# A replanned instruction order, key-row sums in halves, and GpSimd waiting for small VectorE groups, in a fused attention and expert kernel

## The chip, the cores and the metric

The kernel runs on 1 core of one Trainium2 chip. The metric is the device time of one execution in microseconds (us), as the median over several executions. Engines: TensorE (PE in the profile; PEld is its weight load), VectorE (DVE), ScalarE (ACT), GpSimd (POOL), and SyncE (SP), which issues most of the DMAs.

## The reference

Four batches of 12,288 query rows (128 wide) attend to 768 keys each. The keys are means over 4x4 patches of `kv`, times `w_sr`, and they are the values too. The result feeds a mixture of 8 experts in which each row uses its best expert alone:

```python
kv_pool = kv.reshape(B, H // r, r, W // r, r, C).mean(axis=(2, 4))
k = v = kv_pool.reshape(B, -1, C) @ w_sr
s = scale * (q @ k.transpose(0, 2, 1))
a = softmax(s);  x = (a @ v).reshape(B * S, D)
logits = x @ w_gate;  e = argmax(logits);  gate = softmax(logits)[e]
y = gate[:, None] * (relu(x @ w1[e]) @ w2[e])
```

## The kernel before

The queries are cut into 96 blocks of 512 rows (24 for each batch), numbered t. For a block the kernel computes:

- scores: 3 pairs of 512-column matmuls (`s`), ScalarE's exponential (`e`, line 974) and a VectorE operation of 1024 columns (`r`, line 976) which takes e away from 1 + s;
- values: 36 small matmuls into `po` from `r` and from a 128x128 matrix `M` of the batch;
- `x` in two float16 parts: either ScalarE (line 1010) and VectorE (1011) make them, or ScalarE copies `po` (1013) and GpSimd makes both parts (1014, 1016); a transposing DMA turns them (1022);
- the hidden layer of the one expert that the batch is guessed to use: three units of 128 hidden columns (`ph`), ScalarE's ReLU (1045, 1053), the first unit split in two parts by GpSimd (1047, 1049);
- the output `py`: for each of 4 chunks of 128 rows, 3 matmuls with `L`, 2 with the split unit, and one for each unit used; VectorE applies the gate (1080), and a DMA stores.

The queries' own two parts are made by GpSimd (955, 957) and turned by a DMA (959).

For a third unit there is a choice for each block, the way `u{t}`. Without it, the unit's four output matmuls are made. With it, they are left out (`UB = UH - 1`), and ScalarE's ReLU of that unit also sums its result into a flag (line 1057, with an extra instruction that reads the accumulator), which later decides whether the block's rows stand. Other ways choose the engine of one copy: `x{t}` for the two parts of `x`, `l{t}` for the logits' copy (ScalarE line 1018 or VectorE line 1020), `a`, `b`, `c` for the key parts and weights of a batch.

Once per batch there is other work among the blocks. `keys` loads 12 pieces of `kv`; GpSimd adds four rows of each of 3 groups (`rows_sum`, line 443, 1024 columns each; batches 1 to 3 only), halves them twice more (447, 455), and PE turns and multiplies them. `expert` guesses the expert (576 to 580), makes gate weights relative to it (`relative`, 584 to 588), loads the two weights (625, 626), and sorts and gathers hidden units in many small steps. `marks` and `count_steps` (1421 to 1424) gather the rows that the shortcut does not cover; `general_step` can compute 128 such rows exactly, and is placed once after each of the first three batches.

The order of all of it is made by a planner, `Plan`, when the kernel is built. Each `op(engine, us, fn, at, needs, gives, bufs, ...)` has a length `us`, a due time `at`, its needs, and its buffers. `order` simulates the engines with these lengths: at every step it takes, of the operations that can start, the earliest by start and due time. `NUDGE` moves due times, of a kind of operation, of one operation (`=name`) or of one block (`@t`); `WAYS` makes the choices above. An operation with `lock`, and every GpSimd operation, also holds one common lock in the plan, so that no two of these overlap there:

```python
if o.lock:
    start = max(start, locked)
```

`issue` then emits the instructions in the planned order. On the chip each engine runs its instructions in that order, and waits only where data or a buffer demands it: the lock is in the plan alone. Early in the plan (20 to 110 us) PE's empty places are filled with matmuls without use (`fill`, on `slots16`).

Of the kernel before, what the change touches and what calls it, by code (L numbers as in the profile page):

```python
# [17 lines left out]
P = 128  # L18
# [55 lines left out]
pf.48:14.5 pf.72:-14 pl:-52 po.1:1 po.2:0.5 pooled.2:3.5 pt.2.3:4 qh:1.5 qp:2.5 quiet.72:-41.5 r.0:-1 r.1:2.5 r.2:-3
see:-10 some0:20 uy0:-53 vTd.0:11.5 w:-9.5 w2U:11 w2m:-8.5 xf:0.5 xh:0.5 zp:2.5 =D.15:9 =Mh.0:11 =e.23.1:-4.5
=e.36.2:1 =e.38.1:-0.5 =e.38.2:-8.5 =e.49.2:12 =e.5.2:-88.5 =e.52.2:-5.5 =e.54.1:4.5 =e.63.2:-1.5 =e.66.1:-8
=e.67.2:-6 =e.79.1:-23 =e.8.0:10 =e.85.2:-0.5 =e.88.2:3.5 =ex.1:1.5 =ex.8:2 =fl.1:38 =fl.27:4 =fl.56:-21 =fl.75:5
=fl.79:-1.5 =g.2:-1.5 =g.5:10.5 =g.7:-8 =g.71:-6.5 =g.73:-26.5 =gate.12:3 =gate.22:-2 =general.0.done:-5.5
=general.0.s:-3.5 =general.1.ph0:-2 =general.1.ph4:-11 =general.2.find:-0.5 =general.2.h0:-23 =gf.47:1.5 =gf.57:-3.5
=gf.65:-0.5 =gh.3:5.5 =gh.35:3.5 =kp0.2:10 =kt.0:47 =kv.0.2.3:-11.5 =lg.56:-5 =lg.75:-1.5 =lg.76:-5.5 =lg.79:-4.5  # L80
=lgc.10:4.5 =lp.0.0:21.5 =lp.1.24:18 =own2.2:-2 =pL.0:-2.5 =pX.0:-6.5 =perm.2.1:2 =perm.2.4:-1.5 =ph.0.1:5 =ph.0.2:4.5
=ph.16.1:1.5 =ph.21.1:-10.5 =ph.25.1:1 =ph.25.2:-12 =ph.26.0:3 =ph.43.1:0.5 =ph.44.1:8 =ph.48.0:-3 =ph.48.1:-2
=ph.49.1:-8.5 =ph.51.0:6 =ph.52.2:-2 =ph.62.0:-2.5 =ph.79.0:1 =ph.79.1:3 =ph.8.2:-1 =ph.80.2:3.5 =ph.81.0:1 =ph.88.1:1
# [5 lines left out]
=s.21.2:3 =s.22.0:2.5 =s.22.1:-1.5 =s.3.0:-12.5 =s.31.1:-5 =s.32.2:2 =s.33.0:9.5 =s.33.2:-6.5 =s.44.2:-8 =s.46.0:-5.5
=s.52.0:8 =s.61.0:-3 =s.71.0:-2.5 =s.78.2:-6 =s.81.0:-2 =s.88.1:-4.5 =s.88.2:-5.5 =s.9.1:-6 =s.91.1:-2.5 =s.94.1:7  # L90
=s.95.0:-9 =s.95.1:-1.5 =s.95.2:3.5 =se.13:15.5 =some.2:2.5 =unit.3:22.5 =w.7:20.5 =w2l.2:-7.5 =xf.60:6.5 =xf.77:4
=xf.80:2 =xf.88:-11 =xh.29:-18.5 =xh.52:10 =xl.21:5.5 =xl.68:6 =xl.81:28 =xl.87:-10 =ys.10:-5 =ys.20:-32.5 =ys.30:2
=ys.67:3.5 =ys.75:-2.5 @0:1.5 @1:-7.5 @14:-0.5 @15:1 @20:-1.5 @21:1.5 @23:0.5 @24:1 @26:-6 @3:-0.5 @30:-1.5 @31:2
# [3 lines left out]
""".split())}
WAYS = dict.fromkeys("""
a0 a1 a2 b2 c1 c2 c3 l3 l4 l9 l11 l13 l16 l17 l19 l21 l22 l23 l31 l33 l34 l36 l37 l38 l42 l45 l46 l48 l49 l50 l56 l59
l60 l61 l62 l69 l75 l78 l80 l81 l82 l83 l84 l85 l87 l88 l89 l93 u0 u1 u4 u5 u12 u13 u14 u15 u16 u19 u23 u25 u27 u31  # L100
u32 u34 u35 u37 u38 u39 u41 u43 u45 u46 u48 u49 u50 u51 u52 u53 u55 u56 u57 u62 u63 u64 u65 u72 u75 u78 u79 u80 u82
u84 u85 u86 x0 x7 x8 x9 x13 x17 x18 x19 x20 x21 x22 x24 x30 x31 x32 x34 x36 x37 x39 x41 x42 x43 x44 x45 x51 x54 x55
x57 x60 x62 x63 x64 x66 x67 x69 x70 x71 x74 x76 x77 x78 x79 x80 x82 x84 x88 x94
# [12 lines left out]
class Plan:  # L116


    all_ways = False
# [117 lines left out]
@with_exitstack
def attention_moe(ctx: ExitStack, tc, q, kv, w_sr, w_gate, w1, w2, out):
# [164 lines left out]
    def keys(b, when):  # L403
# [6 lines left out]
        for d in range(NK // D):  # L410
# [123 lines left out]
        op("POOL", 1.75, lambda: nc.gpsimd.tensor_sub(kp.tile[:, 1], kt.tile, kp.tile[:, 0]), at + 5, [("kp0", b)],  # L534
# [16 lines left out]
        op("DVE", .3, lambda: nc.vector.scalar_tensor_tensor(M.tile[:, 1, :P], pm.tile[:, :P], cn[:, 9:10], M.tile[:, 0, :P],  # L551
# [11 lines left out]
    def expert(b, at):  # L563
# [3 lines left out]
        op("DVE", .25, lambda: nc.vector.tensor_scalar(cbc.tile, ones, cn[:, 7:8], None, op0=ALU.mult), at,  # L567
# [22 lines left out]
        op("DVE", 1.0, guess, at + .5, [("pg", b)], [("first", b)], [pg, cg])  # L590
        op("DVE", 1.0, relative, at + 2, [("first", b)], [("cg", b)], [cg], lock=True)
# [28 lines left out]
        op("DVE", .4, logits_m, at + 4, [("plg", b), ("M", b)], [("Mx", b), ("v16x", b)], [plg, M])  # L620
# [41 lines left out]
        op("DVE", .5, sides, at + 8.5, [("zc", b)], [("side", b)], [pz, sg])  # L662
# [16 lines left out]
        op("DVE", .8, near, at + 11.5, [("u2", b), ("mir", b)], [("key", b)], [pu, sg], lock=True)  # L679
# [24 lines left out]
        op("DVE", .17, lambda: chosen(0), at + 15, [("less", b, 0)], [("some0", b)], [la, sg])  # L704
        op("DVE", .35, largest, at + 16, [("less", b, 1), ("some0", b)], [("some", b)], [la, sg])
# [48 lines left out]
        op("DVE", .35, limit, at + 35, [("class", b), ("unit", b)], [("Tb", b)], [la])  # L754
# [28 lines left out]
        op("DVE", .85, scales, at + 16, [("pw", b)], [("ws0", b)], [pw, ws])  # L783
        op("POOL", 1.1, scales2, at + 17, [("ws0", b), ("mir", b)], [("ws", b)], [ws, sg])
# [709 lines left out]
```

## Time and profile before

| what | value |
|---|---|
| median of 3 executions | 817.34 us (816.2 to 818.12) |
| profiled execution, its own time | 819.5 us |
| its span, first to last instruction | 817.7 us |
| mean granted TensorE clock | 0.987 |
| PE busy | 759.8 us (93%) |
| VectorE busy | 652.2 us (80%) |
| GpSimd busy | 601.1 us (74%) |
| ScalarE busy | 592.2 us (72%) |

Busy times are sums over the whole span. TensorE's matmuls overlap each other, so that its busy share is no utilization; the granted clock is a share of full speed.

### The profile page before, as it was taken

Reading aid. Unit: us, or ns where it says so; the run is one execution under the profiler, and the core shown is the slowest. Engines: PE = TensorE matmul, PEld = TensorE weight load, DVE = VectorE, ACT = ScalarE, POOL = GpSimd, SP = SyncE. Lnnn points to the kernel's source line nnn. Section 1 sums busy time; section 2 is a strip of 40 time slices with the busy share of each in tenths; the row PEclk is TensorE's granted clock in tenths of the full one; section 3 lists DMA queues with packets and bytes.
Section 4 is the critical chain, followed back from the end, with each engine's and each line's share of the span. In section 5 each row is a group of like instructions: output and inputs, shape, how many; then the busy total and the mean of one; then the engine's idle time right before and its main releaser. Section 6 shows DMA issues by size and latency. Waiting matters only on the chain.

```text
span 817.7 us, 21949 instructions
## 1 busy us (share of the span) xinstructions
PE 759.8 (93%) x8535; PEld 597.3 (73%) x8535; DVE 652.2 (80%) x1224; ACT 592.2 (72%) x949; POOL 601.1 (74%) x802
## 2 busy tenths in 40 slices
PE   5978999999998988999998978999999999999996
PEld 4547777788786766788776756787787777787875
DVE  5767876888877988878979888788896899868684
ACT  1435878778788766877878767888878878788773
POOL 0543599976779978996778788987767888566545
PEclk9989999999999999999999999999999999999999
DMA  9642999894589987897659789979467789757543
GB/s 338 207 99 53 185 210 256 185 208 103 111 212 173 240 201 190 201 172 169 118 138 218 161 208 222 233 166 202 109 127 153 162 165 226 147 116 136 126 84 93
DMA packets 328282, 139.45 MB, mean 171 GB/s; under 512 B 214590, under 2 KB 320194, under 8 KB 328176
## 3 DMA queue, kind: packets, MB, share of 16 engines
q1 hardware_dynamic: 327696, 137.80, 76.4%
q8 instruction: 67, 1.10, 0.6%
q14 instruction: 39, 0.32, 0.1%
q0 software_dynamic: 192, 0.17, 0.1%
q10 hardware_dynamic: 288, 0.07, 0.0%
HBM read 59.12 MB, written 26.94 MB: 105 GB/s over the span
## 4 chain that ended last, share of the span: by engine, by line
PE 62%; DVE 18%; DMA 7%; POOL 6%; issue 3%; ACT 3%; SPq 0%; DVEq 0%; POOLq 0%; ACTq 0%
PE b L353 30%; PE po L353 17%; PE s L353 13%; DVE r L976 8%; DMA qT<-qp 4%; DMA kv<-in_kv_dram 2%; POOL kv L443 2%; DVE y L1080 1%; ACT e L974 1%; DVE junk L1181 1%; DVE xp L1011 1%; POOL g L1049 1%; DMA x<-xp 1%; DVE la L698 1%; DVE PU L746 0%
## 5 line engine op out<-in xcount | busy, mean ns | idle before, releaser
L976 DVE SCALAR_TENSOR_TENSOR r<-s,e 128x1024 bf16<-128x1024 f32 x288 | 346.2, 1215 | 66.5 <-ACT e L974 64.7
L974 ACT ACTIVATE e<-s 128x1024 f32<-128x1024 f32 x288 | 292.5, 1026 | 95.8 <-PE s L353 88.1
L353 PE MATMUL po<-v,r 128*128 128x145 f16 x2304 | 253.7, 228 | 6.7 <-DVE xp L1011 3.2
L353 PE MATMUL s<-qT,KT 128*128 128x512 f16 x576 | 170.5, 384 | 20.1 <-DVE r L976 12.7
L353 PEld LDWEIGHTS <-r 128*128 128x128 bf16 x2304 | 169.1, 99 | 26.9 <-DVE xp L1011 3.8
L353 PE MATMUL b<-w2U,g 128*128 128x128 f16 x1736 | 159.8, 219 | 1.0 <-POOL g L1049 1.0
L353 PE MATMUL b<-x,w1U 128*128 128x512 f16 x465 | 141.9, 381 | 4.2 <-ACT g L1053 1.4
L353 PE MATMUL po<-M,qT 128*128 128x136 f16 x1152 | 131.8, 224 | 0.0
L353 PE MATMUL b<-L,x 128*128 128x128 f16 x1116 | 123.0, 219 | 0.6 <-ACT pT L467 0.3
L1053 ACT ACTIVATE g<-b,zb 128x512 f16<-128x512 f32 x146 | 99.4, 689 | 25.8 <-PE b L353 24.9
L1049 POOL TENSOR_TENSOR g<-X,g 128x512 f16<-128x512 f32 x96 | 112.8, 1175 | 6.5
L957 POOL TENSOR_TENSOR qp<-qr,qp 128x512 f16<-128x512 f32 x94 | 110.4, 1175 | 5.3
L353 PEld LDWEIGHTS <-g 128*128 128x128 f16 x1736 | 113.0, 98 | 1.2 <-POOL g L1049 1.1
L353 PEld LDWEIGHTS <-qT 128*128 128x128 f16 x1152 | 85.4, 98 | 32.2 <-issue 6.9
L353 PEld LDWEIGHTS <-x 128*128 128x128 f16 x1116 | 81.0, 98 | 17.8 <-issue 2.8
L1047 POOL CAST g<-X 128x512 f16<-128x512 f32 x96 | 60.8, 634 | 41.5 <-ACT X L1045 37.5
L353 PEld LDWEIGHTS <-KT 128*128 128x128 bf16 x576 | 51.2, 100 | 53.4 <-issue 23.2
L955 POOL CAST qp<-qr 128x512 f16<-128x512 f32 x94 | 59.1, 630 | 36.7 <-DMA qr<-in_q_dram 25.2
L1080 DVE TENSOR_TENSOR y<-b,gt 128x512 f32<-128x512 f32 x96 | 65.3, 681 | 17.8 <-PE b L353 12.7
L1045 ACT ACTIVATE X<-b,zb 128x512 f32<-128x512 f32 x96 | 66.4, 693 | 16.8 <-PE b L353 16.1
L353 PEld LDWEIGHTS <-w1U 128*128 128x128 f16 x480 | 45.6, 99 | 35.5 <-issue 4.3
L443 POOL TENSOR_TENSOR kv<-kv,kv 128x1024 f32<-128x1024 f32 x27 | 63.6, 2356 | 6.3 <-DMA kv<-in_kv_dram 5.4
(365 smaller groups left out, 992.3 us busy)
## 6 DMA issues: line engine op xcount, KB each, us to landing
qr<-in_q_dram SPq DMA_DIRECT2D x96, 256.0 KB, 3.4
out_dram<-y SPq DMA_DIRECT2D x96, 256.0 KB, 2.8
kv<-in_kv_dram SPq DMA_DIRECT2D x41, 512.0 KB, 6.5
raw<-in_moe_w_dram SPq DMA_DIRECT2D x14, 512.0 KB, 5.5
e<-in_kv_dram SPq DMA_DIRECT2D x3, 512.0 KB, 8.6
v_dram<-vT SPq DMA_DIRECT2D x4, 384.0 KB, 2.9
qT<-qp SPq DMA_TRANSPOSE x94, 3.4
x<-xp SPq DMA_TRANSPOSE x93, 3.5
```

The costliest lines, as they stand in the source:

```text
L353: return nc.tensor.matmul(o, l, r, start=start, stop=stop)
L443: nc.gpsimd.tensor_add(flat(to), flat(to), flat(of))
L698: nc.vector.tensor_scalar(lc(2 + NC * j, NC), limits, lc(j), key(j), op0=ALU.is_ge, op1=ALU.mult)
L955: op("POOL", .62, lambda: nc.gpsimd.tensor_copy(qp.tile[:, 0], qr.tile), T - 1.9 * LEN, [("qr", t)], [("qh", t)], [qr, qp])
L957: op("POOL", 1.17, lambda: nc.gpsimd.tensor_sub(qp.tile[:, 1], qr.tile, qp.tile[:, 0]), T - 1.8 * LEN, [("qh", t)], [("qp", t)], [qr, qp])
L974: op("ACT", 1.03, lambda e=e, ps=ps: nc.scalar.activation(e.tile, ps.tile, AF.Exp), at + .6, [("s", t, s)], [("e", t, s)], [ps, e])
L976: op("DVE", 1.22, lambda e=e, ps=ps, s=s: nc.vector.scalar_tensor_tensor(r.tile[:, 2 * s:2 * s + 2], ps.tile, 1.0, e.tile, op0=ALU.add, op ...
L1045: op("ACT", .69, lambda ph=ph, zu=zu: nc.scalar.activation(gf.tile, ph.tile, AF.Relu, bias=zu()), at + .5, [("ph", t, u), ("zb", b)], [("g ...
L1047: op("POOL", .62, lambda: nc.gpsimd.tensor_copy(gg.tile[:, 0], gf.tile), at + 1.5, [("gf", t)], [("gh", t), ("g", t)], [gf, gg])
L1049: op("POOL", 1.16, lambda: nc.gpsimd.tensor_sub(gg.tile[:, UH], gf.tile, gg.tile[:, 0]), at + 2, [("gf", t), ("gh", t)], [("g", t)], [gf, gg])
L1053: op("ACT", .69, lambda u=u, ph=ph, zu=zu: nc.scalar.activation(gg.tile[:, u], ph.tile, AF.Relu, bias=zu()), at + .5, [("ph", t, u), ("zb" ...
L1080: op("DVE", .69, lambda: nc.vector.tensor_tensor(y.tile, py.tile.rearrange("p (c d) -> p c d", d=C), bc(gr["gt"].tile[:, 0, js], C), op=AL ...
```

## The change

Five things are changed together.

- Many lengths `us` in the plan are replaced by others (some 40 of them), and many groups of small VectorE instructions get `lock=True`.
- `rows_sum` adds 512 columns at a time, twice, instead of 1024 once.
- `issue` adds a real wait: where a locked VectorE operation has more than one instruction, the first GpSimd operation planned after it waits for the last of them, if its planned start lies no later than 2.5 us after the group's planned end.
- The plan lets `ph` of the later units wait for its `g` buffer, and `pL` and `Ls` for `Ms`.
- `NUDGE` and `WAYS` are replaced as a whole. Counted from the diff: `u` is set for 62 blocks instead of 46 (17 dropped, 33 new), `x` for 48 instead of 47, `l` for 45 instead of 41; `a` for batches 0 and 1 instead of 0 to 2; `b` for batches 0 and 3 instead of 2; `c` as before.

```diff
 NUDGE = {...}
-L:16 Lh:26 Tb:0.5 cg:-2.5 drs:-8.5 e.1:1.5 e.2:-0.5 ex:4.5 fl:-0.5 gate:6.5 general.0.pl:-39.5 general.0.pv:5.5
...
+D:1.5 KT:-215.5 L:28.5 Lh:-23.5 Mx:-6.5 Tb:2.5 cbc:-20 e.0:-0.5 e.1:0.5 e.2:0.5 fl:-8.5 gate:-1.5 general.0.done:4.5
...
+    FOLLOW = 2.5
...
     def issue(self):
+        block, last = self.tc.nc.cur_bb.bb, None
         for o in self.order():
...
+            n = len(block.instructions)
             o.fn()
+            if o.eng == "DVE" and o.lock:
+                mine = block.instructions[n:]
+                last = (o, mine[-1]) if len(mine) > 1 else None
+            if o.eng == "POOL" and last and o.start < last[0].start + last[0].us + self.FOLLOW:
+                first = next(i for i in block.instructions[n:] if i.engine == mybir.EngineType.Pool)
+                self.tc.add_manual_dep(first, last[1].name, mybir.DependencyInfo(
+                    mybir.DependencyClass.Sync, mybir.DependencyReason.DATA), reason="order")
+                last = None
...
-                def rows_sum(to, of):
-                    flat = lambda t: t.tile.rearrange("p a j c -> p (a j c)")
+                def rows_sum(to, of, a):
+                    flat = lambda t: t.tile[:, a].rearrange("p j c -> p (j c)")
...
-                    op("POOL", 2.5, lambda i=i, raws=raws: rows_sum(raws[0], raws[i]), at + 6 + 2 * n,
...
+                    for a in range(2):
+                        op("POOL", 1.2, lambda i=i, raws=raws, a=a: rows_sum(raws[0], raws[i], a), at + 6 + 2 * n + a / 2,
...
-        op("DVE", 1.0, guess, at + .5, [("pg", b)], [("first", b)], [pg, cg])
-        op("DVE", 1.0, relative, at + 2, [("first", b)], [("cg", b)], [cg], lock=True)
+        op("DVE", 1.07, guess, at + .5, [("pg", b)], [("first", b)], [pg, cg], lock=True)
+        op("DVE", 1.2, relative, at + 2, [("first", b)], [("cg", b)], [cg], lock=True)
...
-        op("POOL", 2.2, lambda: nc.gpsimd.tensor_tensor(rows(w2m.tile), rows(raw[1].tile), bc(col(4), C), op=ALU.mult), at + 15,
+        op("POOL", 1.92, lambda: nc.gpsimd.tensor_tensor(rows(w2m.tile), rows(raw[1].tile), bc(col(4), C), op=ALU.mult), at + 15,
...
             op("PE", .216 if u else .648, hidden, at, [("x", t), ("w1U", b)], [("ph", t, u)],
-               [ph, x, k["w1U"]])
+               [ph, x, k["w1U"]] + [gg] * (u > 0))
...
-            op("DVE", 1.8, count_steps, START + (t + 5) * LEN + 3, [("left", b)], [("steps", b)])
+            op("DVE", 1.1, count_steps, START + (t + 5) * LEN + 3, [("left", b)], [("steps", b)], lock=True)
```

Also given a lock: `sides`, `chosen(0)`, `largest`, `limit`, `biases`, `to_lists`, and in `general_step` `find`, `find2`, `search`, `select` and `weight`. Already locked groups of more than one instruction: `unit_own`, `relative`, `near`, `classes`, `bias`, `constant2`, `equal`.

## Rows read from the trace of the kernel before

**Rows 1.** The page, busy time of each engine: us, share, instructions.
```profile
PE 759.8 (93%) x8535; PEld 597.3 (73%) x8535; DVE 652.2 (80%) x1224; ACT 592.2 (72%) x949; POOL 601.1 (74%) x802
```

**Rows 2.** Windows: length, busy us (instructions) PE, PEld, DVE, ACT, POOL; clock, DMA.
```profile
40.00:60.00 20.00, 14.22 (x86) 8.82 (x85) 13.95 (x15) 7.33 (x12) 10.50 (x10) 0.83 0.52 116
...
100.00:120.00 20.00, 18.69 (x224) 14.36 (x222) 14.67 (x17) 16.07 (x27) 18.61 (x18) 1.00 1.10 216
...
280.00:300.00 20.00, 16.19 (x169) 11.48 (x168) 17.52 (x51) 11.52 (x19) 16.52 (x14) 0.91 0.84 212
...
480.00:500.00 20.00, 18.85 (x204) 14.51 (x202) 17.00 (x37) 14.78 (x27) 18.34 (x21) 0.92 0.77 172
```

**Rows 3.** Timeline of 24 to 60 us: start, us, instruction, [idle before it].
```profile
38.96 4.78 POOL L443 TENSOR_TENSOR kv<-kv,kv 128x1024 f32<-128x1024 f32 x2
...
39.57 1.76 DVE L584 TENSOR_SCALAR cg<-iota_e,con 128x8 f32<-128x8 f32 x1
...
40.59 0.38 SPq L626 DMA_DIRECT2D raw<-in_moe_w_dram  x1
...
41.57 2.19 DVE L586 TENSOR_TENSOR cg<-cg,wg_raw 128x8 f32<-128x8 f32 x1
...
43.80 0.16 DVE L587 TENSOR_REDUCE cg<-cg 128x1 f32<-128x8 f32 x1
43.87 2.33 POOL L443 TENSOR_TENSOR kv<-kv,kv 128x1024 f32<-128x1024 f32 x1
43.99 2.24 DVE L588 TENSOR_SCALAR cg<-wg_raw,cg 128x8 f32<-128x8 f32 x1
...
47.41 1.01 PE L353 MATMUL s<-qT,KT 128*128 128x512 f16 x2 [5.65 <-DVE r L976]
...
55.42 1.89 PE L353 MATMUL b<-con,raw 128*128 128x64 f32 x16
```

**Rows 4.** The page, DMA issues: count, KB each, median us to landing.
```profile
raw<-in_moe_w_dram SPq DMA_DIRECT2D x14, 512.0 KB, 5.5
```

**Rows 5.** Timeline of 281 to 297 us.
```profile
281.39 7.26 POOL L443 TENSOR_TENSOR kv<-kv,kv 128x1024 f32<-128x1024 f32 x3
...
286.47 2.23 DVE L1422 TENSOR_SCALAR steps_i<-steps_i 128x64 int32<-128x64 int32 x1
...
291.87 0.30 PE L353 MATMUL po<-v,r 128*128 128x145 f16 x2 [1.97 <-DVE r L976]
```

**Rows 6.** Timeline of 466 to 480 us.
```profile
475.65 2.33 POOL L443 TENSOR_TENSOR kv<-kv,kv 128x1024 f32<-128x1024 f32 x1
475.77 2.36 DVE L1424 TENSOR_TENSOR_SCAN ends<-steps 128x64 f32<-128x64 f32 x1
...
478.76 0.22 PE L353 MATMUL po<-v,r 128*128 128x145 f16 x1 [2.89 <-DVE xp L1011]
```

**Rows 7.** Two lines: duration ns min/median/max, first and last start.
```profile
L586 DVE TENSOR_TENSOR cg<-cg,wg_raw x4: 166/589/2195, 41.6 to 562.9; 128x8 f32<-128x8 f32 x4
...
L1424 DVE TENSOR_TENSOR_SCAN ends<-steps x4: 291/678/2359, 290.1 to 813.3; 128x64 f32<-128x64 f32 x4
```

**Rows 8.** Chain that ended last: start, us, pieces of matmuls, 32 and 28 each.
```profile
162.90 1.79 PE b L353 x32
...
426.52 1.56 PE b L353 x28
```

**Rows 9.** Lines: group and count, busy us, mean ns, idle before.
```profile
L1049 POOL TENSOR_TENSOR g<-X,g 128x512 f16<-128x512 f32 x96 | 112.8, 1175 | 6.5
...
L443 POOL TENSOR_TENSOR kv<-kv,kv 128x1024 f32<-128x1024 f32 x27 | 63.6, 2356 | 6.3 <-DMA kv<-in_kv_dram 5.4
...
L447 POOL TENSOR_TENSOR kv<-kv 128x512 f32<-128x512 f32 x9 | 12.0, 1336 | 0.5
...
L1057 ACT ACTIVATION_READ_ACCUMULATOR g<-b,zb 128x1 f32 x46 | 9.5, 206 | 0.0
```

**Rows 10.** PE's waits: for what, total us, times, longest us.
```profile
PE s L353 <- DMA qT<-qp: 6.6, 7, 1.7
```

More of the change, by code (lines that the diff above doesn't have):

```diff
@@ L74 @@
[L74 to L83, printed above, removed]
@@ L89 @@
[L89 to L93, printed above, removed]
@@ L94 @@
-@38:-1 @39:-0.5 @4:-3.5 @40:-0.5 @46:-1.5 @47:-1 @5:1.5 @52:1 @55:1 @62:-2 @63:2 @64:0.5 @66:-0.5 @7:3 @72:0.5
-@73:-0.5 @74:1.5 @75:1 @76:-2.5 @77:-1.5 @78:0.5 @79:0.5 @81:-0.5 @82:0.5 @85:1 @87:0.5 @88:-5.5 @89:-7.5 @90:-4.5
-@93:-1.5 @94:2.5
+D:1.5 KT:-215.5 L:28.5 Lh:-23.5 Mx:-6.5 Tb:2.5 cbc:-20 e.0:-0.5 e.1:0.5 e.2:0.5 fl:-8.5 gate:-1.5 general.0.done:4.5
+general.0.ph0:-23 general.0.ph4:-4 general.0.pl:-20 general.1.ph0:-23 general.1.ph4:-9 general.1.pq:22.5
+general.1.pv:8 general.1.py:4 general.2.s:-13 general.2.x:26.5 gf:-1.5 gh:0.5 kp1:-12.5 kv.1.1:-3 kv.1.3:6 less.0:3
@@ new lines @@
+less.1:5 lg:1 lp.0:14.5 lp.48:2.5 mean:-12 mk0.24:-20 mk2.0:40.5 mk2.72:28.5 o:5.5 odd:-6 pL:-3 pX:4 pY:-77.5 pb:-2
+perm.1:-8 perm.2:-4 perm.5:-54.5 pf.72:-26.5 pg:-3 pk.2:-15.5 pk2:-4 pm:15 po.0:1.5 po.2:0.5 pooled.0:-14.5
+pooled.1:1.5 pown:1 pt.0.3:-27 pw:-2 py:9.5 qp:3 r.1:-5.5 r.2:-7.5 rs:-48 s.1:0.5 s.2:0.5 se:-13.5 some:-6.5
+sum.0.2.1:-4 sum.1.2.1:-6 sure.24:2 sure.48:4 u2:-63.5 uy0:-57 v16x:43 w:-14.5 w1l:-5.5 w2l:-10.5 x:11.5 xf:-1 xl:-16
+ys:-5.5 zc:-6.5 zp:26.5 =D.13:-9 =D.7:-3.5 =D.8:8.5 =Lh.0:13 =Mh.0:24 =Tb.3:5.5 =e.15.0:-2 =e.18.2:1.5 =e.33.2:-5.5
@@ new lines @@
+=e.54.2:-5.5 =e.62.2:0.5 =e.66.2:27 =e.69.1:7.5 =e.72.1:9 =e.73.1:-7 =e.75.0:-4.5 =e.9.2:-1 =e.92.1:0.5 =ex.12:9
+=ex.20:11.5 =fl.1:23.5 =fl.26:1.5 =g.15:-5 =g.23:7.5 =g.26:-4.5 =g.27:-11 =g.31:-3.5 =g.42:-10.5 =g.44:2 =g.55:-57.5
+=g.57:-19 =g.90:8 =general.0.ph4:10 =general.0.qt:9.5 =general.1.ph4:-2 =general.1.po:12 =gf.17:-22.5 =gf.22:5
+=gf.37:-13.5 =gf.39:10 =gf.45:-17 =gf.56:3.5 =gf.75:-43.5 =gf.95:-6.5 =gh.25:-4 =gh.27:-4 =gh.28:4.5 =gh.32:2.5
+=gh.52:2.5 =kp1.2:21 =krow.2:-53 =kv.3.1.1:7 =less.0.0:-4.5 =less.0.1:-6 =lg.41:-24.5 =lg.42:5 =lg.65:-4.5 =lg.72:-1.5
@@ new lines @@
+=pt.2.2.3:7 =py.14:11 =py.2:5 =py.25:8 =py.27:8 =py.32:-14 =py.36:5.5 =py.38:-5 =py.56:2 =py.59:1.5 =py.6:-23.5
+=py.77:6 =py.8:-3 =py.81:2 =py.90:0.5 =qh.19:5 =qp.11:1.5 =qp.85:5 =qr.33:-20.5 =r.43.2:1.5 =r.88.2:-6 =s.1.0:2.5
+=s.18.0:-13 =s.2.0:43 =s.2.2:2.5 =s.26.2:-5.5 =s.28.1:-2 =s.30.2:-1 =s.31.1:-6.5 =s.31.2:8 =s.33.2:-4.5 =s.35.2:-3
+=s.44.2:14.5 =s.50.2:-5.5 =s.54.2:-2.5 =s.62.1:3.5 =s.66.2:2 =s.68.0:-14 =s.68.1:-4 =s.77.1:44 =s.79.2:-3 =s.81.1:5
+=s.82.1:-5.5 =s.84.2:-12.5 =s.93.0:-4.5 =top.1.24:-2.5 =w1h.2:12.5 =w1h.3:-5.5 =w2l.3:28.5 =x.46:-5 =x.52:-5
@@ L97 @@
+@91:-7.5 @92:11.5 @93:-2.5 @94:-4 @95:-20.5
 """.split())}
 WAYS = dict.fromkeys("""
[L99 to L102, printed above, removed]
@@ L368, in attention_moe @@
     plan = Plan({**SBUF, **PSUM})
+    plan.tc = tc
     op = plan.op
@@ L499, in rest @@
             nc.gpsimd.tensor_scalar(cn[:, 9:10], cn[:, 8:9], XS, 0.0, op0=ALU.mult, op1=ALU.add)
-        op("DVE", .3, mean, at - 1, [("vTd", b, d) for d in range(KT // 2)], [("mean", b)])
-        op("DVE", .75, unit_own, at, [("mom", b)], [("own", b)], [dg], lock=True)
+        op("DVE", .33, mean, at - 1, [("vTd", b, d) for d in range(KT // 2)], [("mean", b)])
+        op("DVE", .9, unit_own, at, [("mom", b)], [("own", b)], [dg], lock=True)
         op("PE", .1, lambda: mm(pd.tile[:, :P], ones_b, dg.tile, True, True), at + 1, [("own", b)], [("pd", b)],
            [dg, pd])
-        op("DVE", .9, unit, at + 2, [("pd", b), ("mean", b)], [("unit", b)], [pd])
-        op("POOL", .75, rest, at + 3, [("unit", b), "wg"], [("rest", b)])
+        op("DVE", .8, unit, at + 2, [("pd", b), ("mean", b)], [("unit", b)], [pd])
+        op("POOL", .82, rest, at + 3, [("unit", b), "wg"], [("rest", b)])
         KTt = k["KT"] = buf("KT", [P, NK], BF16)
@@ L566, in expert @@
         cbc = buf("cbc", [P, P])
-        op("DVE", .25, lambda: nc.vector.tensor_scalar(cbc.tile, ones, cn[:, 7:8], None, op0=ALU.mult), at,
+        op("DVE", .3, lambda: nc.vector.tensor_scalar(cbc.tile, ones, cn[:, 7:8], None, op0=ALU.mult), at,
            [("unit", b)], [("cbc", b)], [cbc], lock=True)
@@ L677, in near @@
                                            op1=ALU.bitwise_or)
-        op("DVE", .8, near, at + 11.5, [("u2", b), ("mir", b)], [("key", b)], [pu, sg], lock=True)
+        op("DVE", .9, near, at + 11.5, [("u2", b), ("mir", b)], [("key", b)], [pu, sg], lock=True)
         def spread():
@@ L702, in largest @@
             nc.vector.tensor_tensor(lc(2, NC), lc(2, NC), lc(2 + NC, NC), op=ALU.max)
-        op("DVE", .17, lambda: chosen(0), at + 15, [("less", b, 0)], [("some0", b)], [la, sg])
-        op("DVE", .35, largest, at + 16, [("less", b, 1), ("some0", b)], [("some", b)], [la, sg])
+        op("DVE", .27, lambda: chosen(0), at + 15, [("less", b, 0)], [("some0", b)], [la, sg], lock=True)
+        op("DVE", .5, largest, at + 16, [("less", b, 1), ("some0", b)], [("some", b)], [la, sg], lock=True)
         pb = bank()
@@ L752, in limit @@
             nc.vector.tensor_scalar(cn[:, 13:14], cn[:, 3:4], KEYS_MIN, cn[:, 14:15], op0=ALU.is_ge, op1=ALU.mult)
-        op("DVE", .35, limit, at + 35, [("class", b), ("unit", b)], [("Tb", b)], [la])
+        op("DVE", .39, limit, at + 35, [("class", b), ("unit", b)], [("Tb", b)], [la], lock=True)
         wm = buf("u", [P, 2])
@@ L1207, in to_lists, with part @@
             nc.vector.tensor_scalar(left[:, (2 * b + 1) * E:2 * (b + 1) * E], ones[:, :E], pc.tile[:, E:E1], None, op0=ALU.mult)
-        op("DVE", .4, to_lists, at + 11, [("pc", b)], [("left", b)], [pc])
+        op("DVE", .45, to_lists, at + 11, [("pc", b)], [("left", b)], [pc], lock=True)
     def general_step(n=None, at=0.0, follow=()):
         used = {}
-        def part(eng, us, fn, needs, gives, bufs=(), lands=0.0):
+        def part(eng, us, fn, needs, gives, bufs=(), lands=0.0, lock=False):
             if n is None:
@@ L1258, in find2 @@
             nc.vector.tensor_tensor(step, step, u(7), op=ALU.add)
-        part("DVE", 1.6, find, [], "find", [gs, gi, le])
+        part("DVE", 1.3, find, [], "find", [gs, gi, le], lock=True)
         vT = buf("gk", [P, NK])
@@ L1270, in load @@
                               w2[bass.ds(reg_e, 1)].rearrange("o (f p) c -> p (o f) c", p=P))
-        part("SP", 3.2, load, ["find"], "load", [gi, vT, *raw], 4.5)
-        part("DVE", 1.6, find2, ["find"], "find2", [gs, gi, le])
+        part("SP", 2.3, load, ["find"], "load", [gi, vT, *raw], 4.5)
+        part("DVE", 1.5, find2, ["find"], "find2", [gs, gi, le], lock=True)
         NT = NJ + 4
@@ L1290, in search @@
             nc.vector.memset(q_sb(), 0.0)
-        part("DVE", 2.0, search, ["find2"], "search", [gs, gp])
+        part("DVE", 1.7, search, ["find2"], "search", [gs, gp], lock=True)
         pb = tiny([P, 512])
@@ L1302, in select @@
             nc.vector.tensor_tensor(sel0(), sel(), sel0(), op=ALU.subtract)
-        part("DVE", 1.5, select, ["pb"], "select", [gs, gp, pb])
+        part("DVE", 1.6, select, ["pb"], "select", [gs, gp, pb], lock=True)
         pr = tiny([P, 512])
@@ L1353, in general_step @@
         a, aT = buf("row", [P, NK]), buf("gk", [P, KT, P])
-        part("ACT", 1.2, lambda: nc.scalar.activation(a.tile.rearrange("p (h k) -> p h k", h=2), ps.tile[:, :, :KH], AF.Exp,
+        part("ACT", 1.1, lambda: nc.scalar.activation(a.tile.rearrange("p (h k) -> p h k", h=2), ps.tile[:, :, :KH], AF.Exp,
                                                       bias=nmax(), scale=scale, accum_out=sums()), ["top"], "a", [gs, ps, a])
@@ L1383, in choose @@
             nc.vector.tensor_scalar(d(), pl.tile[:, :E], z(1), z(0), op0=ALU.subtract, op1=ALU.mult)
-        part("DVE", 1.95, choose, ["pl", "a"], "d", [gs, gi, g, pl])
+        part("DVE", 1.82, choose, ["pl", "a"], "d", [gs, gi, g, pl])
         part("ACT", .5, lambda: nc.scalar.activation(d(), d(), AF.Exp, scale=wg_st[:, 1:2], accum_out=z(2)), ["d"], "ex", [gs, g])
@@ L1391, in weight @@
             nc.vector.tensor_tensor(z(3), z(0), z(2), op=ALU.mult)
-        part("DVE", .7, weight, ["ex"], "w", [gs])
+        part("DVE", .58, weight, ["ex"], "w", [gs], lock=True)
         h = buf("gp", [P, NF, TAIL])
```

78 lines of the change are left out of this document (45 added, 33 removed).

## The prediction

> **What bounds the kernel now.** Read the page's busy times first [rows 1]. PE stands at 93%, the next engine at 80%, so PE is the bound on average; but its busy time counts overlapped matmuls, and the share says nothing about single stretches. So take the windows next [rows 2] and look for those in which PE falls off and the granted clock falls too. From 40 to 60 us PE is busy 14.22 of 20 us at a clock of 0.83, from 280 to 300 us 16.19 at 0.91, from 480 to 500 us 18.85 at 0.92. [...] What it takes from PE is the missing share of the clock times the window: (1 - 0.83) x 20 = 3.4 us, then 1.8 and 1.6.
>
> [...] At 38.96 GpSimd starts two additions of key rows; three VectorE instructions of 8 columns take 1.76, 2.19 and 2.24 us, and the last ends when GpSimd's third addition does (43.99 + 2.24 = 46.23, 43.87 + 2.33 = 46.20) [rows 3]. At 286.47 an instruction of `count_steps` takes 2.23 us and ends at 288.70, GpSimd's three additions at 288.65 [rows 5]. At 475.77 one takes 2.36 us and ends at 478.13, GpSimd's addition at 477.98 [rows 6]. The second and the last of these lines, 586 and 1424, take 166 and 291 ns at their shortest [rows 7]. So a small VectorE instruction which starts during a GpSimd addition is held to its end, and what is queued behind it on VectorE is late: PE then waits 5.65, 1.97 and 2.89 us [rows 3, 5, 6].
>
> **The change, part by part.** Sums are made against the profiled execution's own 819.5 us (span 817.7, and 1.8 around it); it stands 2.2 us above the median of 817.3, and the last step takes these off.
>
> *Ways.* Sixteen more blocks drop the third unit's four output matmuls. A block's output takes 1.79 us with 32 matmuls and 1.56 with 28 [rows 8], 0.23 less, so PE loses 16 x 0.23 = 3.7 us of work. Bounds: 0, if every such block waits for something else; 3.7 if PE is the bound around all of them. I take 3.7, since most windows have PE nearly full. ScalarE reads 16 more accumulators, 16 x 0.206 = 3.3 us [rows 9], spread over 800; its idle quarter hides them [rows 1], and without that cover they would cost 3.3. The other ways move one block's `x` parts to GpSimd, four small copies to VectorE, and a few key copies between ScalarE and GpSimd: some us each way on engines with 20% and more idle, so nothing.
>
> *Holds.* The new wait keeps GpSimd's next planned operation behind the last instruction of a small group, and the new locks let the plan leave room for it. Where it works, three holds go:
> - 475 us: PE's wait of 2.89 and 1.6 of clock, 4.5 at most, 0 at least (VectorE's `xp` could be late for another reason). I take 3.5, near the top, as nothing but the held scan stood ahead of `xp` on VectorE.
> - 290 us: 1.97 and 1.8 of clock, 3.8 at most, 0 at least. I take 3: GpSimd's own lateness there (three additions in one piece, 7.26 us) is only partly cured.
> - 40 us: 5.65 and 3.4 of clock, 9.1 at most. The weights were asked for at 40.59 and land in 5.5 (median), so at about 46, an estimate; PE first uses them at 55.42, 9 us later [rows 3, 4]. But part of PE's queue there is filler, whose slowness costs nothing by itself, and key loads and block 0's other needs may be late next; 0 at least. I take 4, somewhat under the middle.
>
> *Halves.* 27 additions of 2356 ns become 54 [rows 9]. None of the new shape is in the trace. Its nearest rows are GpSimd's two-input operations of 512 columns, 1175 ns with a float16 result and 1336 with a float32 one over strided rows; two make 2350 to 2672, so between nothing and 0.32 us more each, 0 to 8.5 in all. I take half, 4 us, and it is hidden in GpSimd's 26% idle [rows 1]; uncovered, each of the 9 chains of three sums would pass on up to 0.95. What is bought: no single hold is longer than half as long, also for groups of one instruction, which the wait doesn't protect, and other GpSimd work can go between the halves.
>
> *The wait's own price.* By the diff 68 groups can be followed by a waiting GpSimd operation (13 in each batch, one more in the last, 15 in the general steps). A wait puts GpSimd behind whatever VectorE has queued ahead of the group, and behind GpSimd's waiting operation stand the `g`, `qp` and `xp` parts, for which PE waits, the last two by way of a transposing DMA. Nothing of this is in the trace. Below: 0, since GpSimd would be held or idle anyway. Above: as in the slower rival below. I take 2, near the bottom, since GpSimd is idle for a quarter of the run [rows 1].
>
> [...] The reduction at 43.80 took 0.16 us while a GpSimd addition began beside it at 43.87; the instruction of two inputs before it was held [rows 3]. [...]
>
> *Order.* NUDGE and the lengths reorder everything, and no row prices that. Bounds from the nearest row: a late `qT`, 1.7 us at its longest [rows 10], and as much again of clock, 3.4 either way. Since new stalls are likelier where nothing was stalled, I take 1.5 of loss.
>
> Sum: -3.7 - 3.5 - 3 - 4 + 2 + 1.5 = -10.7, 819.5 - 10.7 = 808.8, less 2.2 is 806.6, say **807 us**. Own range of this case: all top gains, 3.7 + 4.5 + 3.8 + 9.1 = 21.1, give 796; the work alone without the holds' gain, less the 2 of the wait, 816.
>
> **Rivals.**
> - *The holds go but something else is late at the same places.* For it: from 480 to 500 us GpSimd is busy 18.34 of 20 us [rows 2], and at 281 its additions alone take 7.26 [rows 5], so `g` would still be late. At the start the weights may not be the next limit. Then only PE's work is saved, and 2 lost: 817.3 - 3.7 + 2 = 815.6, about **815**. Against it: VectorE is named as what ended PE's waits in all three [rows 3, 5, 6].
> - *Slower: GpSimd starves behind its waits.* In stretches such as 100 to 120 us GpSimd is busy 18.61 of 20 [rows 2] and can't make up a wait. If VectorE is late itself, GpSimd stands for a group and the operation ahead of it, then `qp` and so `qT` come late, and PE loses up to 1.7 and as much of clock, 3.4 each [rows 10]. Four such new stalls use up the gain of 12.7 that I count before the wait's price and its 2; with six the time is 817.3 - 10.7 - 2 + 20.4 = **825**. Against it: 817.7 - 601.1 = 216.6 us of GpSimd are idle over the run [rows 1].
> - *Much faster: the new lengths let the plan avoid most other waits too.* PE's waits for `qT` (6.6 us [rows 10]) would go as well, beside all top gains: 817.3 - 21.1 - 6.6 = 790 at best, with a few us of the wait's price some **793**.
> - *No change to speak of:* gains and new stalls cancel, **817**.
>
> **How the numbers follow.** About 0.2% (1.6 us) is what a measurement here can tell from none. Forecast 0.56 (796 to 816); the holds replaced 0.14 (815, of which a third falls within 0.2%); much faster 0.08; no change 0.08; slower 0.14. Faster: 0.56 + 0.09 + 0.08 = 0.73, and 0.02 of the no-change case lies just past the bound, 0.75; same 0.11; slower 0.14. The range runs from 796 to 818.5: it leaves out the slower case and half of the much faster one.
>
> **What would show it.** Right: no VectorE instruction under 130 columns above 1.3 us; no clock fall near 290 and 479; the first expert weights used before 51 us; 64 fewer matmuls with `w2U`; GpSimd's idle time put down to small VectorE lines, with PE's waits for `qT` and `g` not grown. Wrong: PE's waits on `qT`, `x` or `g` grown by over 8 us in total, more clock falls than four before the end, or halves well over 1.34 us each.

## The result and the profile after

The changed kernel takes 810.62 us in the median of 20 executions (806.64 to 816.35), the kernel before, on the same chips, 818.51 us (813.63 to 823.38). The ratio is 0.9905, with a 95% interval of 0.9883 to 0.9926: 0.95% faster, 7.8 us of 818.5. The forecast was 807 us against 817.3, a ratio of 0.987; the measured time lies in its range, and the gain is three quarters of the one forecast. The profiled execution has a span of 805.7 us and is one of the quick ones; the sums below go by ratios, on 818 us.

The page of the changed kernel, the engines' busy times, and of its groups the output matmuls and the key additions (line numbers are some 20 higher now; busy us, mean ns, idle before):

```profile
PE 750.6 (93%) x8477; PEld 591.9 (73%) x8477; DVE 631.1 (78%) x1227; ACT 591.4 (73%) x961; POOL 604.4 (75%) x831
...
L374 PE MATMUL b<-w2U,g 128*128 128x128 f16 x1672 | 157.1, 220 | 0.5 <-POOL g L1072 0.5
...
L465 POOL TENSOR_TENSOR kv<-kv,kv 128x512 f32<-128x512 f32 x54 | 68.2, 1285 | 10.2 <-DVE gp L1325 5.9
```

Against [rows 1], VectorE is busy 21 us less, though it has three instructions more. There are 64 output matmuls less (1736 stood in the page before). A half of a key addition takes 1285 ns. The windows of the changed kernel:

```profile
40.00:60.00 20.00, 19.65 (x162) 15.75 (x160) 15.24 (x30) 10.47 (x17) 14.29 (x19) 1.00 0.53 129
...
280.00:300.00 20.00, 16.36 (x188) 12.45 (x186) 16.52 (x44) 15.03 (x26) 13.81 (x20) 1.00 0.81 190
...
480.00:500.00 20.00, 15.01 (x173) 11.99 (x171) 13.46 (x36) 11.81 (x21) 14.16 (x20) 0.91 0.85 196
```

From 40 to 60 us PE is busy 19.65 us instead of 14.22, at the full clock [rows 2]. The clock still falls once between 480 and 500 us (0.91). The timeline of the changed kernel, 36 to 50 us, shows the start's group as it is now:

```profile
39.21 0.47 DVE L607 TENSOR_SCALAR cg<-iota_e,con 128x8 f32<-128x8 f32 x1
...
39.72 0.17 DVE L608 SCALAR_TENSOR_TENSOR cg<-cg 128x8 f32<-128x8 f32 x1
39.92 0.17 DVE L609 TENSOR_TENSOR cg<-cg,wg_raw 128x8 f32<-128x8 f32 x1
...
40.32 0.23 DVE L611 TENSOR_SCALAR cg<-wg_raw,cg 128x8 f32<-128x8 f32 x1
...
40.61 0.24 POOL L633 COPY v<-extra 128x54 f16<-128x54 f16 x1 [0.96 <-DVE cg L611]
40.80 5.09 POOL L465 TENSOR_TENSOR kv<-kv,kv 128x512 f32<-128x512 f32 x4
...
45.91 1.89 PE L374 MATMUL b<-con,raw 128*128 128x64 f32 x16
```

GpSimd stands for 0.96 us until line 611 ends, and starts its additions after it; the group takes 1.3 us instead of 6.7 [rows 3]. The first expert weights are used at 45.91 instead of 55.42; how much of this is the wait's, and how much the new order's, the first experiment tells. The same two lines as in [rows 7], in the changed kernel:

```profile
L609 DVE TENSOR_TENSOR cg<-cg,wg_raw x4: 166/166/169, 39.9 to 546.1; 128x8 f32<-128x8 f32 x4
```
```profile
L1447 DVE TENSOR_TENSOR_SCAN ends<-steps x4: 291/291/291, 274.7 to 800.9; 128x64 f32<-128x64 f32 x4
```

The median and the longest have come down to the shortest: no execution of these lines is held any more. PE's own waits (us, times, longest):

```profile
PE s L374 <- DVE r L999: 9.2, 13, 1.5
PE s L374 <- DMA qT<-qp: 7.5, 5, 3.3
```

### The profile page after: what moved, and what is told of

It is laid out like the page before. It is cut to its first block, busy times and chain, and to the rows that moved or that the text cites. A ratio compares the mean times of both kernels' runs of the same rounds, so it can differ in the third digit from the quotient of the medians.

```text
span 805.7 us, 21920 instructions
## 1 busy us (share of the span) xinstructions
PE 750.6 (93%) x8477; PEld 591.9 (73%) x8477; DVE 631.1 (78%) x1227; ACT 591.4 (73%) x961; POOL 604.4 (75%) x831
## 4 chain that ended last, share of the span: by engine, by line
PE 70%; DVE 9%; DMA 7%; POOL 6%; ACT 4%; issue 3%; SPq 0%; POOLq 0%; DVEq 0%; ACTq 0%
PE b L374 35%; PE po L374 19%; PE s L374 14%; DMA qT<-qp 4%; DVE r L999 4%; POOL kv L465 2%; ACT e L997 2%; DMA kv<-in_kv_dram 1%; POOL g L1072 1%; DVE y L1103 1%; DMA gp<-in_q_dram,gi 1%; ACT g L1076 1%; DMA kr<-kp 1%; DVE xp L1034 1%; POOL g L1070 1%
## 5 line engine op out<-in xcount | busy, mean ns | idle before, releaser
L374 PE MATMUL po<-v,r 128*128 128x145 f16 x2304 | 249.2, 227 | 2.9 <-ACT X L1036 1.5
L374 PE MATMUL s<-qT,KT 128*128 128x512 f16 x576 | 166.8, 379 | 19.2 <-DVE r L999 9.2
L374 PEld LDWEIGHTS <-r 128*128 128x128 bf16 x2304 | 167.4, 98 | 20.1 <-issue 1.3
L374 PE MATMUL b<-w2U,g 128*128 128x128 f16 x1672 | 157.1, 220 | 0.5 <-POOL g L1072 0.5
L374 PEld LDWEIGHTS <-g 128*128 128x128 f16 x1672 | 110.3, 98 | 0.7 <-POOL g L1072 0.7
L1076 ACT ACTIVATE g<-b,zb 128x512 f16<-128x512 f32 x130 | 88.4, 687 | 28.4 <-PE b L374 24.4
L465 POOL TENSOR_TENSOR kv<-kv,kv 128x512 f32<-128x512 f32 x54 | 68.2, 1285 | 10.2 <-DVE gp L1325 5.9
```

Of the source, the lines that this page charges most:

```text
L374: return nc.tensor.matmul(o, l, r, start=start, stop=stop)
L1076: op("ACT", .69, lambda u=u, ph=ph, zu=zu: nc.scalar.activation(gg.tile[:, u], ph.tile, AF.Relu, bias=zu()), at + .5, [("ph", t, u), ("zb" ...
```

## The experiments

Each ratio is to the kernel before on the same chip, with its 95% interval; 0.001 is 0.82 us. It is not the quotient of the two medians, which differs from it by up to 0.0034; where a reading hangs on that, both are given.

**The wait alone taken out of the changed kernel (a_nowait).**

```diff
-            if o.eng == "POOL" and last and o.start < last[0].start + last[0].us + self.FOLLOW:
+            if self.WAIT and o.eng == "POOL" and last and ...:   # WAIT = False
```


> The changed kernel with its plan, order and halves, but GpSimd waits for no VectorE group. My theory (the wait is what ends the holds; the plan's locks alone are not kept by the chip): holds of over 1 us on small VectorE instructions come back near 40, 290 and 475 us, about half as long as before since the additions are halves; the gain of the holds, 8.5 us net of the wait's price, shrinks to about 3: time 5 to 6 us above the changed kernel, ratio to the kernel before 0.997. Rival (the new plan alone keeps the two engines apart): the same as the changed kernel, 0.990 +- 0.003. Rival (the wait costs more than it gives): faster than the changed kernel, under 0.987.

Measured: 819.15 us, ratio 1.0034 (1.0011 to 1.0057). Without the wait nothing is left of the gain; it is worth 1.0034 - 0.9905 = 0.0129, 10.5 us, in this order. The plan's locks alone do not keep the engines apart. Timeline of this kernel, VectorE's count of the steps, GpSimd's operations beside it, and PE behind it:

```profile
273.73 3.85 POOL L466 TENSOR_TENSOR kv<-kv,kv 128x512 f32<-128x512 f32 x3
...
276.43 1.20 DVE L1446 TENSOR_SCALAR steps_i<-steps_i 128x64 int32<-128x64 int32 x1
...
277.53 1.16 POOL L1073 TENSOR_TENSOR g<-X,g 128x512 f16<-128x512 f32 x1
277.66 1.08 DVE L1447 CAST steps<-steps_i 128x64 f32<-128x64 int32 x1
...
278.64 1.27 POOL L470 TENSOR_TENSOR kv<-kv 128x512 f32<-128x512 f32 x1
278.78 1.28 DVE L1448 TENSOR_TENSOR_SCAN ends<-steps 128x64 f32<-128x64 f32 x1
...
281.23 0.59 PE L375 MATMUL s<-qT,KT 128*128 128x512 f16 x2 [2.68 <-DVE r L1000]
```

Each is held, no longer for 2.3 us but to the end of one short GpSimd operation, one after the other, and PE waits 2.68 us behind them. At the start it is different: there the group of `relative` takes 1.9 us without the wait (39.62 to 41.51), one instruction of it is held (1.04 us, 0.23 with the wait), the weights are used at 46.63, and the clock does not fall (1.00 from 40 to 60 us). The gates' multiplication (x96: shortest, median and longest ns; start of the first and the last), without the wait and with it:

```profile
L1104 DVE TENSOR_TENSOR y<-b,gt x96: 627/682/693, 100.0 to 810.5; 128x512 f32<-128x512 f32 x96
```
```profile
L1103 DVE TENSOR_TENSOR y<-b,gt x96: 627/684/693, 97.9 to 799.3; 128x512 f32<-128x512 f32 x96
```

So in the new order the wait gives 2.1 us up to the first block and 11.2 up to the last. Block by block, in these two executions, the lead stays near 2 us until the count of the steps near 280 us, is 5 behind it, 6.9 from 400 to 478 us without a rise near 475, and grows after that. Most of the start's gain in the changed kernel thus came with the new order and the halves.

**The wait alone put into the kernel before (b_waits),** behind the same groups (but `equal`, which runs once), in the old order, with whole additions.

```diff
+            if o.eng == "DVE" and (o.lock or g in self.GROUPS):   # g: the name of the group
+                mine = block.instructions[n:]
+                last = (o, mine[-1]) if len(mine) > 1 and g in self.GROUPS else None
+            if o.eng == "POOL" and last and o.start < last[0].start + last[0].us + self.FOLLOW:
+                (the wait, as in the change)
```


> The kernel before, in its own order, with the real wait of the change alone: behind the same groups of small VectorE instructions, GpSimd's next planned operation waits for the last of the group. My theory: the three holds go, the first expert weights are used near 47 us instead of 55, and the time falls by 8.5 us (10.5 of holds less 2 of price), ratio 0.990. Rival (GpSimd starves, as its order was not planned with these waits): PE's waits for qT and g grow by over 8 us, ratio 1.000 or above.

Measured: 808.32 us, ratio 0.9912 (0.9876 to 0.9947; the medians, against 817.62, give 0.9886): the whole gain of the change, from one of its five parts. Timeline, 36 to 52 us:

```profile
38.71 1.37 DVE L600 TENSOR_SCALAR cg<-iota_e,con 128x8 f32<-128x8 f32 x1
...
41.03 4.79 POOL L459 TENSOR_TENSOR kv<-kv,kv 128x1024 f32<-128x1024 f32 x2 [0.97 <-DVE cg L604]
...
47.53 1.89 PE L368 MATMUL b<-con,raw 128*128 128x64 f32 x16
```

The additions of 1024 columns are still there, and begin 2 us later than in [rows 3]; the group is held once, at its first line (1.37 us, to 40.08), by what GpSimd had begun before (1.65 us from 38.41, to 40.06). The weights are used at 47.53.

**Whole additions in the changed kernel's order (a_whole).**

```diff
-                    flat = lambda t: t.tile[:, a].rearrange("p j c -> p (j c)")
-                    nc.gpsimd.tensor_add(flat(to), flat(to), flat(of))
+                    flat = lambda t: t.tile.rearrange("p a j c -> p (a j c)")
+                    if a == 1:
+                        nc.gpsimd.tensor_add(flat(to), flat(to), flat(of))
```


> The changed kernel with its order, but each sum of key rows is made as one addition of 1024 columns where the second half stood; nothing where the first stood. My theory: GpSimd saves 27 x 0.21 = 5.8 us of its own time, which was hidden anyway, and single VectorE instructions can be held up to 2.36 us again: 0 to 3 us slower than the changed kernel, ratio 0.990 to 0.994. Rival (the finer pieces are what lets g and qp through): 5 us or more slower, 0.997.

Measured: 809.96 us, 0.9912 (0.9882 to 0.9942). With the wait in place the halves are worth nothing that can be measured.

**Halves alone in the kernel before (b_halves),** two additions of 512 columns, one right after the other.

> The kernel before with each addition of key rows made as two of 512 columns, one right after the other, and no wait. My theory: GpSimd is 6 us longer busy, hidden; a held VectorE instruction waits 1.3 us instead of 2.4, so the three holds are about halved and the run is 3 to 5 us faster, ratio 0.994 to 0.996. Rival (the next half starts before VectorE's next instruction does, so a group is held piece by piece as long as before): 1.000 +- 0.003.

Measured: 815.57 us, 0.9975 (0.9943 to 1.0007). The interval holds both no change and the 3 to 4 us of the theory's nearer end. Its timeline, 36 to 50 us, shows the group held piece by piece, as the rival says, though not for as long as before:

```profile
43.49 4.94 POOL L444 TENSOR_TENSOR kv<-kv,kv 128x512 f32<-128x512 f32 x4
44.11 0.68 DVE L585 TENSOR_SCALAR cg<-iota_e,con 128x8 f32<-128x8 f32 x1
44.83 1.19 DVE L586 SCALAR_TENSOR_TENSOR cg<-cg 128x8 f32<-128x8 f32 x1
46.05 1.19 DVE L587 TENSOR_TENSOR cg<-cg,wg_raw 128x8 f32<-128x8 f32 x1
...
47.27 0.16 DVE L588 TENSOR_REDUCE cg<-cg 128x1 f32<-128x8 f32 x1
...
47.47 0.99 DVE L589 TENSOR_SCALAR cg<-wg_raw,cg 128x8 f32<-128x8 f32 x1
...
49.64 0.59 PE L353 MATMUL s<-qT,KT 128*128 128x512 f16 x2 [3.26 <-DVE r L977]
```

Four of the group's five instructions are held by one half each, the reduction is not: 4.3 us for the group instead of 6.7, and PE waits 3.26 us instead of 5.65.

**The start's wait alone (b_wait_start):** in the kernel before, only behind `relative` of batch 0.

```diff
+                last = (o, mine[-1]) if len(mine) > 1 and o.gives[0] == ("cg", 0) else None
```


> The kernel before with one real wait: behind the five small VectorE instructions that make the gate weights of batch 0 relative (near 40 us), GpSimd's next planned operation waits for the last. My theory (the start's hold is paid by the whole run, since PE has little idle time later): with all waits block 0's output came 6.8 us earlier; with this one it comes 6 to 7 us earlier and the run is 5 to 7 us faster, ratio 0.992 to 0.994. Rival (block 0 may come earlier, but its gain is given back at a later limit, and the gain of all waits came from the many small ones): 2 us or less, ratio 0.998 or above.

Measured: 812.49 us, 0.9912 (0.9876 to 0.9947), 7.2 us from one wait; the medians, against 817.47, give 5.0 us. The gates' multiplication (x96: shortest, median and longest ns; start of the first and last), first of the kernel before, then of this one:

```profile
L1080 DVE TENSOR_TENSOR y<-b,gt x96: 621/682/693, 101.6 to 811.7; 128x512 f32<-128x512 f32 x96
```
```profile
L1096 DVE TENSOR_TENSOR y<-b,gt x96: 620/681/693, 96.7 to 804.3; 128x512 f32<-128x512 f32 x96
```

The first block comes 4.9 us earlier, less than the 6 to 7 expected, the last 7.4: the start's gain is not given back on the way. That the ratio is the one of all waits does not make the two equal: by the medians all waits give 9.3 us and this one 5.0. With all waits the last block comes 14.2 us earlier.

**The waits behind the lists and the step counts alone (b_wait_steps),** at some 286, 474, 670 and 812 us.

> The kernel before with real waits behind two groups of each batch alone, the ones that copy the lists and count the steps (near 286, 474, 670 and 812 us). My theory: the holds at 286 and 475 us go, 3 and 3.5 us by the prediction; ratio 0.992 to 0.994. Rival (the gain of the one at 475 is given back at the next late transfer, as the run with all waits suggests: 20 us ahead in block 48, 14 in block 56): only the one at 286 stays, 3 to 4 us, ratio 0.995 to 0.997.

Measured: 813.54 us, 0.9941 (0.991 to 0.9972), 4.8 us (3.9 by the medians) for four places, not the two that the prediction priced; the interval does not tell the two sizes apart.

**Both of these and no other (b_wait_two).**

> The kernel before with the real waits behind the start's group (batch 0's relative gate weights) and behind the groups that copy lists and count steps, and nowhere else. My theory: the two gains, 0.9912 and 0.9941 when made alone, come from different places of the run and add, 0.985; then the other waits of the change cost some 5 us, since all of them give 0.9912. Rival (a gain made at the start is partly given back at the later places, as the clock falls only move): 0.990 or above, like all waits.

Measured: 808.16 us, 0.9858 (0.9798 to 0.9918): the two gains add, 0.0088 + 0.0059 = 0.0147 against 0.0142. Set against the 0.9912 of all waits, the others would cost 0.0054, 4 us; but the intervals overlap, and the medians (8.8 us here, 9.3 with all waits) show no cost, so whether the other waits cost or give anything stays open. **With halves as well (b_halves_two):**

> The kernel before with halves and with the waits of the run b_wait_two. My theory: with the main holds gone the halves add little, ratio within 0.003 of that run, 0.985. Rival (groups without a wait are held often enough that halves are worth 3 us more): 0.981.

Measured: 807.71 us, 0.9855 (0.9801 to 0.9909). Halves add nothing here either. These two have the lowest ratios of all kernels run; their intervals overlap the changed kernel's, and by the medians (0.9892 and 0.9886) they do not differ from the kernel with all waits (0.9886).

**The order alone (a_order):** the changed kernel without the wait, with whole additions, and with 16 of the 33 newly set blocks making their third unit's output matmuls again.

```diff
-                op("PE", .223 * (5 + UB), lambda UB=UB: rows(UB), Hh + 4.2,
+                op("PE", .223 * (5 + UB), lambda UB=UB: rows(UH if t in (2, 10, 17, 21, ..., 83, 88) else UB), Hh + 4.2,
```


> What is left of the change without three of its parts: the new order and lengths, but no real wait, whole additions of key rows, and 16 of the 33 newly set blocks make their third unit's output matmuls, so that as many do as before. My theory by now (the new order is no gain in itself): 1.0034 for the changed kernel without the wait, and 16 of the 62 blocks' 0.0207 on top, 1.0087, 7 us slower than the kernel before. Rival (halves and blocks don't add up with the order; the order alone is as good as the old one): 1.000 +- 0.003.

Measured: 825.23 us, 1.0089 (1.0055 to 1.0124). The new order, with the new lengths, is 7.3 us slower than the old one; the parts add up as expected.

**More and less work on PE.** a_third: all 62 blocks make the third unit's output matmuls, in the changed kernel's order.

> The changed kernel with its order, but the 62 blocks that leave out the third unit's four output matmuls make them after all, and ScalarE reads no accumulator for them: 248 matmuls more on PE (62 x 0.23 = 14.3 us), 62 x 0.2 = 12.4 us less on ScalarE. My theory (PE bounds nearly every stretch, so 16 blocks were worth 3.7 us): 14 us slower than the changed kernel, ratio 1.007. Rival (a fair part of the blocks waits for something else): 5 us slower or less, 0.997 or below.

Measured: 825.3 us, 1.0112 (1.0075 to 1.0149): 0.0207 or 17 us more for 248 matmuls, of which 14.3 are their own time. The other way, b_waits_u: the kernel before with all waits, and all 92 blocks that may leave the matmuls out do so.

> The kernel before in its own order with the real waits, and all 92 blocks that may do so leave out the third unit's four output matmuls (46 more than before; ScalarE reads 46 more accumulators, 9.5 us). My theory (PE bounds nearly every stretch, 15 us for 62 blocks): 46 x 0.25 = 11.5 us faster than with the waits alone, ratio 0.977, the fastest of all. Rival (ScalarE, with longer work than its order was planned for, makes PE wait): half of that or less, 0.984 or above.

Measured: 812.83 us, 0.9944 (0.9911 to 0.9978), no faster than the waits alone (0.9912). And a_u: the changed kernel with the last 30 blocks leaving theirs out.

> The changed kernel with its order, waits and halves, and the 30 blocks that still make the third unit's output matmuls leave them out too (120 matmuls less, 30 accumulator reads more). My theory after the run b_waits_u (work taken from PE comes back only until the next late transfer, and each clock fall eats 1.7 us or more): 0 to 5 us faster than the changed kernel, ratio 0.985 to 0.9905. Rival (PE-bound throughout): 7.5 us faster, 0.981.

Measured: 815.92 us, 0.9987 (0.9961 to 1.0013), 6.7 us slower than the changed kernel with 120 matmuls less. Both theories miss (of b_waits_u the rival's number, 0.984 or above, came), but neither run is a test of the matmuls alone, because both edits also change the order. They make the sum of the flags need the flags of all blocks in the plan, and the planner then places other operations anew. SyncE issues 459 DMAs in every kernel here; in a_u 99 of them stand at another place of the sequence than in the changed kernel, in b_waits_u 87 at another than in the kernel before, and in each of the other experiments none, against the kernel that it was made from. PE's timeline in a_u:

```profile
510.16 1.46 PE L374 MATMUL s<-qT,KT 128*128 128x512 f16 x3 [6.39 <-DMA qT<-qp]
```

One late transfer, 6.39 us, and a granted clock of 0.52 behind it, from 510.16 to 514.40 us ((1 - 0.52) x 4.24 = 2.0), are 8.4 us, more than the 30 blocks' matmuls take (30 x 0.23 = 6.9 us). Whether the transfer is late by the new places of the DMAs was not tried. ScalarE's longer work, the rival named for b_waits_u, shows in one of the two: PE's waits for ScalarE, summed, are 16.0 us in a_u against 11.0 in the changed kernel, but 8.4 in b_waits_u against 8.8 in b_waits.

## Why the prediction was right

*The holds* were the cause that it named, and the wait ends them. No VectorE instruction under 130 columns takes over 1.16 us in the changed kernel (2.36 in the kernel before), the falls of the clock near 290 and 479 us (0.76 from 290 to 294 us and 0.60 from 480 to 484) are gone (1.00 from 260 to 495 us), the weights are used at 45.91, before 51 us; only PE's waits for `qT` grew a little, from 6.6 to 7.5 us. Summed over the rows of the view of PE's waits, PE stands for VectorE 33.1 us in the kernel before and 21.7 with the wait alone put in, 33.1 in the changed kernel without the wait and 23.7 with it. Priced at 10.5 us for three holds less 2 for the wait, the wait gave 7.2 us in the old order and 10.5 in the new one. Between the places the sizes were off: in the old order the start's hold, put at 4 us of a possible 9.1, gave 7.2 (5.0 by the medians), and the wait behind lists and steps, with 6.5 put on two of its places, gave 4.8. In the new order the wait gives 2.1 us up to the first block, some 3 near 280 us, as forecast for that place, and nothing near 475; that its total of 10.5 lies near the 8.5 forecast is in part luck, as the rest arises at places that the prediction did not price.

*The order* is the step that failed: the term of 1.5 us was mis-sized. The new NUDGE, ways and lengths without the other parts lose 7.3 us. That the sum still came out near the time is due to two errors that partly cancel: measured, 7.3 for the order, -4.5 for 16 blocks and the halves (a_order to a_nowait), -10.5 for the wait, -7.7 in all; forecast, 1.5, -3.7 and -8.5, -10.7. The bounds of that term, 3.4 either way from one late `qT`, were too narrow for an order replaced as a whole.

*Ways.* Sixteen blocks were priced at 3.7 us and gave about 4.5 with the halves, in an order planned for them. The reason given, that PE bounds nearly every stretch, agrees with a_third, where 14.3 us of matmuls cost 17; a_u and b_waits_u can neither confirm nor refute it, since their order changed too.

*Halves.* 4 us more of GpSimd were forecast, 4.6 came (68.2 against 63.6 us [rows 9]), hidden as forecast (0.9905 with halves, 0.9912 with whole additions in a_whole).

*The rivals.* GpSimd does wait longer for VectorE through the wait: summed over its waits, 93 us in 69 places in b_waits against 75 in 46 in the kernel before, and 73 in 59 in the changed kernel against 54 in 42 without the wait. But what it waits for ScalarE and for DMAs falls by more, from 104.5 to 73.1 us and from 100.1 to 79.5, so that the price is covered, as the prediction argued for its lower bound. GpSimd starved at one place, named by its waits in the changed kernel:

```profile
POOL kv L465 <- DVE gp L1325: 5.9, 1, 5.9
```

There an addition stands behind `select` of a general step, which itself waits for PE and for the step's earlier parts. The rival of something else that is late came true at one of the three places: near 491 us, 16 us behind the hold that went, the changed kernel has a stall in PE's and SyncE's timelines (the first two lines SyncE's, the last PE's):

```profile
486.70 0.39 SPq L1292 DMA_DIRECT2D raw<-in_moe_w_dram  x1
487.21 3.60 SPq L982 DMA_TRANSPOSE qT<-qp  x1
```
```profile
495.00 0.60 PE L374 MATMUL s<-qT,KT 128*128 128x512 f16 x2 [3.29 <-DMA qT<-qp]
```

The transpose of a block's queries was issued right behind the general step's weights, and PE uses them 7.8 us later (3.4 is the median to landing); whether the weights delay them is not shown. With the clock at 0.66 from 495 to 499 us, 1.4 us, this stall costs 4.7, as much as the hold at 475 us was priced at most, 4.5. The reduction of the group took 0.16 us amid GpSimd's halves in b_halves, where the four others were held (0.68, 1.19, 1.19 and 0.99 us), as it took 0.16 beside an addition in the kernel before [rows 3]; why it was not held, no run shows. The wait's own price, put at 2 us, no run shows by itself: b_wait_two has few waits and is as fast as b_waits (0.9858 and 0.9912, the medians 0.9892 and 0.9886), and no run tells what the others cost.

## What to carry to other kernels

A planner's rule that two engines must not overlap did not keep them apart on the chip (the scan of 64 columns took 1.28 us in a_nowait) until a real wait did (0.29 us in the changed kernel); when a tiny instruction takes as long as another engine's big one and ends with it (2.36 and 2.33 us [rows 6]), order the two for real, and start with the places where a chain stands behind it: the waits at the start and behind lists and steps, nine in all at most, gave here what all 68 at most gave. Test the parts of a bundle one by one, by taking each out of the new kernel and putting each into the old one: here one part carried the whole gain, and a new order that was made along with it took some of it back. Look whether an edit leaves the order as it was before its time is put down to the edit: two that were to price matmuls had moved the DMAs as well.

## What the runs showed of the hardware

- Halving GpSimd's additions did not halve the hold of a group: the next small instructions, but for the reduction, were each caught by the next half (1.19, 1.19 and 0.99 us in b_halves), 4.3 us instead of 6.7 for five instructions.
- Making GpSimd wait for VectorE added 18 us of such waiting in the old order (93 against 75) and 19 in the new (73 against 54), and took more than that from its waits for ScalarE and DMAs (31 and 21 us).
